# Splitting the second product's weights one group later, and making three operands before the second layer begins

## The chip, the cores and the metric

The kernel runs on one core of a Trainium2 chip. The metric is the device time of one execution in microseconds (us). Five engines work side by side, each through its own queue in order: TensorE (PE, with its weight loads shown as PEld), VectorE (DVE), ScalarE (ACT), GpSimd (POOL) and SyncE (SP), which issues nearly all DMAs. They meet through semaphores.

## The reference

The input passes through three layers:

```python
def _attn_ref(q, k, v, w_phi):           # linear attention, 4 x 8 heads of 576 x 64
    ...
    return (num / den).astype(np.float32)
def _moe_ref(x, w_in, w_out):            # 2304 x 512, d_ff 2048: the first layer below
    h = x @ w_in
    return np.maximum(0.01 * h, h) @ w_out
def _moe2_ref(x, domain_probs, w1, w2):  # 4 experts, F = 1024: the second layer below
    p = domain_probs / (domain_probs.sum(-1, keepdims=True) + 1e-09)
    for e in range(4):
        h = np.maximum(x @ w1[e], 0.0)
        out += p[:, e:e + 1] * (h @ w2[e])
```

Everything is float32. Each float32 operand of a matmul is split in two parts, a rounded high part ("hi", made on ACT) and the rest ("lo", a subtraction on DVE or POOL), and a product is three matmuls: hi by hi, hi by lo, lo by hi.

## The kernel before, in words

**Layout in time.** Attention and the first layer run mixed over the 4 batches, ordered by a written plan and the planner's own estimate. The first layer's last group, `moe1_group(16)`, holds only its "down" products: 8 pieces of 12 matmuls. Then comes the second layer, 48 groups `group(k)`, k = 16 j + c: three blocks j of 768 tokens, in each 16 slices c of 256 columns of w1.

**A group.** The product x @ w1 of a slice is done as 7 products of half size instead of 8 (Strassen's scheme: sums of blocks of x, `x2_steps`, by sums of blocks of w1, `w2_sums`). `product(k, i, ...)` is 6 matmuls of 384 columns, into PSUM tiles X, V and Y; ACT copies X to Y (line 804) before product 2 goes on in X. `relu_hi` (ACT) and `relu_lo` (DVE) make the operand of the second product. This second product, `down(k - 1, i)`, i = 0 to 5, belongs to the group before and stands between the products of group k: 6 matmuls of 512 columns each, then an add into the output by DVE (line 774). PE's order in a group: products 1, 5, down 3, products 2, 6, down 4, products 3, 7, down 5, down 0, product 4, down 1, down 2. Everything in `kept(...)` keeps the order in which it is written on its engine; DMAs and the first layer's work are placed by the planner.

**Weights of the first product.** `w2_dma` loads a slice of w1 (tile r), `w2_sums` makes 4 sums on POOL, `w2_hi` and `w2_lo` split them on ACT and POOL. This is done in group k for group k + 1.

**Weights of the second product.** `w2_dma_d` loads 2 x 256 KB of w2 into the tile r2, of which there is one (bufs 1). `w2_hi_d` (ACT, line 707) and `w2_lo_d` (POOL, line 711) split it into `wd[k]`, of which there are two (bufs 2). Before the change group k splits wd[k + 1], behind `relu_lo(k, 3, Z)` and ahead of down 5 of group k - 1. wd[k + 1] lies in the buffer of wd[k - 1], which down 3, 4, 5, 0, 1 and 2 of group k - 1 read in this same group.

**Sums of x.** A block needs 7 operands, in `XOPS` order b11, t1, b21, t2, b22, t3, t4. Those called b are split as they are; those called t need a subtraction first (line 616), then the hi part (ACT, line 638) and the lo part (line 639). For blocks 1 and 2 the subtractions run on POOL, one operand as the `fill` of groups c = 1, 3, 5, 7, 9, 11 and 15 of the block before. For block 0 they run on DVE: four are spread over the last batch of the first layer, b22 stands in the first layer's last group, and t3 and t4 (`extra`) inside group 0. Group 0 has no down products.

Of the kernel before, what the change touches and what calls it, by code (L numbers as in the profile page):

```python
# [75 lines left out]
NC2 = NE * FF2 // 256  # L76
# [3 lines left out]
def body(ctx, tc, kT, qT, vh, w_phi, w_in, w_out, probs, w1, w2, out):  # L80
# [504 lines left out]
    def pieces(*halves):  # L585

        cuts = sorted({0, TH} | {S - t0 % S for t0 in halves if S - t0 % S < TH})
        return [
            (o, e - o, [((t0 + o) // S, (t0 + o) % S) for t0 in halves])
            for o, e in zip(cuts, cuts[1:])  # L590
        ]
# [3 lines left out]
    def x2_steps(j):  # L595

        T = (2 * TH * j, 2 * TH * j + TH)
        kind = ([xp, xp, xp, 0, 0], [0, xp, xp, xp, xp], [xp, xp, xp, 0, 0])[j]
        slots, raw = [], []
        xops[j] = {}  # L600

        def half(i):
            if i % 3 == 0:
                pool = kind[i // 3] or x2p[0]
                slots.append(pool.tile([128, 3, 2, TH], F32R, tag="x", name="xo"))
            return slots[i // 3][:, i % 3]

        def part(d, t, o, n):
            b, s = t
            return accs[b][:, 2 * d : 2 * d + 2, s : s + n]  # L610

        eng = nc.vector if j == 0 else nc.gpsimd

        def diff(out, f, g, halves):
            for o, n, at in pieces(*halves):
                kept(eng.tensor_tensor(
                    out=out[:, :, o : o + n], in0=f(o, n, at), in1=g(o, n, at), op=ALU.subtract
                ))

        def step(i, name):  # L620
            if name[0] == "t":
                if not raw:
                    raw.append((x2p[0] if j else xp).tile([128, 3, 2, TH], F32, tag="x", name="xt"))
                r = raw[0][:, {"t1": 0, "t2": 1, "t3": 2, "t4": 0}[name]]
                of = {
                    "t1": (lambda o, n, at: part(0, at[1], o, n), lambda o, n, at: part(0, at[0], o, n), T),
                    "t2": (lambda o, n, at: part(1, at[0], o, n), lambda o, n, at: raw[0][:, 0, :, o : o + n], T[1:]),
                    "t3": (lambda o, n, at: part(1, at[0], o, n), lambda o, n, at: part(0, at[0], o, n), T[1:]),
                    "t4": (lambda o, n, at: part(1, at[0], o, n), lambda o, n, at: raw[0][:, 1, :, o : o + n], T[:1]),
                }[name]  # L630
                diff(r, *of)
                src = [(0, TH, r)]
            else:
                d, t = int(name[1]) - 1, T[int(name[2]) - 1]
                src = [(o, n, part(d, at[0], o, n)) for o, n, at in pieces(t)]
            hi, lo = half(2 * i), half(2 * i + 1)
            for o, n, r in src:
                kept(nc.scalar.copy(out=hi[:, :, o : o + n], in_=r))
                kept(eng.tensor_tensor(
                    out=lo[:, :, o : o + n], in0=r, in1=hi[:, :, o : o + n].bitcast(F32), op=ALU.subtract  # L640
                ))
            xops[j][name] = hi, lo

        return [lambda i=i, name=name: step(i, name) for i, name in enumerate(XOPS)]
# [8 lines left out]
    def kept(ins):  # L653

        if "h" in m2:
            tc.keep_in_program_order(ins)
        return ins
# [4 lines left out]
    def w2_dma(c):  # L662

        pool, tag = (m2["r"], "r") if m2 else (wp, "w")
        r = pool.tile([128, 4, 256], F32, tag=tag, name="r")
        nc.sync.dma_start(out=r[:, 2:4].rearrange("p a f -> p (a f)"), in_=w1[2 * c])
        nc.sync.dma_start(out=r[:, 0:2].rearrange("p a f -> p (a f)"), in_=w1[2 * c + 1])
        return r

    def w2_sums(r):  # L670
        pool, tag = (m2["r"], "r") if m2 else (wp, "w")
        s = pool.tile([128, 4, 256], F32, tag=tag, name="rs")
        for o, x, y, op in (
            (s[:, 0], r[:, 0], r[:, 1], ALU.add),
            (s[:, 1], s[:, 0], r[:, 2], ALU.subtract),
            (s[:, 2], r[:, 2], r[:, 0], ALU.subtract),
            (s[:, 3], r[:, 3], s[:, 1], ALU.subtract),
        ):
            kept(nc.gpsimd.tensor_tensor(out=o, in0=x, in1=y, op=op))  # L679
        return s  # L680

    def w2_dma_d(c):
        r2 = m2["r2"].tile([128, 2, DM], F32, tag="r2", name="r2")
        for t in range(2):
            nc.sync.dma_start(out=r2[:, t], in_=w2[2 * c + t])
        return r2

    def w2_operands(k):
        if m2:
            wo[k] = [m2["wu"].tile([128, 7, 256], F32R, tag="wu", name=n) for n in ("wuh", "wul")]  # L690
        else:
            wo[k] = [xp.tile([128, 7, 256], F32R, tag="x", name=n) for n in ("wuh", "wul")]
# [12 lines left out]
    def w2_hi_d(k, r2):  # L705
        wd[k] = m2["wd"].tile([128, 2, 2, DM], F32R, tag="wd", name="wd")
        kept(nc.scalar.copy(out=wd[k][:, 0], in_=r2))  # L707

    def w2_lo_d(k, r2):
        d = wd[k]  # L710
        kept(nc.gpsimd.tensor_tensor(out=d[:, 1], in0=r2, in1=d[:, 0].bitcast(F32), op=ALU.subtract))  # L711
# [19 lines left out]
    def relu_hi(k, at, src):  # L731
        kept(nc.scalar.activation(out=gs2[k][0][:, at], in_=src, func=AF.Relu))  # L732
# [46 lines left out]

        return evict  # L780

    def group(k, r, r2, fill, extra):

        gs2[k] = [m2["h"].tile([128, 4, TH], F32R, tag="h", name=n) for n in ("gh", "gl")]
        X = m2["px"].tile([128, 512], F32, tag="x", name="px")[:, 0:TH]
        V = m2["pv"].tile([128, 512], F32, tag="v", name="pv")[:, 0:TH]
        Z = m2["pz"].tile([128, 512], F32, tag="z", name="pz")[:, 0:TH]  # L790
        Y = m2["y"]
        ss = m2["sum"].tile([128, 2, TH], F32, tag="s", name="s")
        if k == 0:

            kept(nc.tensor.matmul(
                Y, lhsT=wo[k][0][:, 1, 0:128], rhs=xops[0]["b11"][0][:, 0], start=True, stop=True
            ))
        more = r is not None
        run = lambda f: f and f()
        if more:  # L800
            s = w2_sums(r)
            w2_operands(k + 1)
        product(k, 1, X, True)
        kept(nc.scalar.copy(out=Y, in_=X))  # L804
        product(k, 5, V, True)
        kept(nc.scalar.copy(out=ss[:, 0], in_=V))
        if more:
            w2_hi(k + 1, r, s, 0)
            w2_lo(k + 1, r, s, 0)
        run(down(k - 1, 3))  # L810
        for f in extra[:1]:
            f()
        product(k, 2, X, False)
        relu_hi(k, 0, X)
        relu_lo(k, 0, X)
        product(k, 6, Y, False)
        kept(nc.scalar.copy(out=ss[:, 1], in_=Y))
        if more:
            w2_hi(k + 1, r, s, 1)
            w2_lo(k + 1, r, s, 1)  # L820
        run(down(k - 1, 4))
        for f in extra[1:]:
            f()
        product(k, 3, V, False)
        kept(nc.vector.tensor_tensor(out=V, in0=V, in1=ss[:, 1], op=ALU.add))
        relu_hi(k, 1, V)
        product(k, 7, Y, False)
        kept(nc.vector.tensor_tensor(out=Z, in0=Y, in1=ss[:, 0], op=ALU.add))
        relu_lo(k, 1, V)
        relu_hi(k, 3, Z)  # L830
        relu_lo(k, 3, Z)
        if more:
            w2_hi_d(k + 1, r2)
            w2_lo_d(k + 1, r2)
        run(down(k - 1, 5))
        run(down(k - 1, 0))
        run(fill)
        product(k, 4, Y, False)
        relu_hi(k, 2, Y)
        relu_lo(k, 2, Y)  # L840
        run(down(k - 1, 1))
        run(down(k - 1, 2))
# [12 lines left out]
    for b in range(B):  # L855
# [5 lines left out]
        else:  # L861
            early = x2_steps(0)
# [11 lines left out]
    r = w2_dma(0)  # L874
# [3 lines left out]
        w2_hi(0, r, s, i)  # L878
        w2_lo(0, r, s, i)
    for i, f in enumerate(G[2:]):  # L880
        if i == 2:
            early[4]()
        f()
    left0.close()
    for name, bufs in (("r", 2), ("r2", 1), ("wu", 4), ("wd", 2), ("sum", 2), ("h", 4)):
# [3 lines left out]
        m2[name] = opened(left, name, bufs, space=bass.MemoryType.PSUM)  # L889
    m2["y"] = m2["py"].tile([128, 512], F32, tag="y", name="py")[:, 0:TH]  # L890
    n = NB * NC2
    r2 = w2_dma_d(0)
    r = w2_dma(1)
    w2_hi_d(0, r2)
    w2_lo_d(0, r2)
    nxt = []
    for k in range(n):
        j, c = divmod(k, NC2)
        if c == 0 and j + 1 < NB:
            nxt = x2_steps(j + 1)  # L900
        r2 = w2_dma_d((k + 1) % NC2) if k + 1 < n else None
        fill = nxt.pop(0) if nxt and (c % 2 == 1 and c < 12 or c == NC2 - 1) else None
        group(k, r, r2, fill, early[5:] if k == 0 else [])
        r = w2_dma((k + 2) % NC2) if k + 2 < n else None
    for i in (3, 4, 5, 0, 1, 2):
        down(n - 1, i)()
    left.close()
# [34 lines left out]
```

## Time and profile before

| | us |
|---|---|
| median of 3 runs | 1461.37 |
| lowest and highest | 1460.64, 1462.51 |
| the profiled execution's own time | 1460.94 |
| its span in the trace | 1459.2 |
| first matmul of the second layer, from the span's start | 641.08 |

The busy shares of the whole span are PE 94%, DVE 56%, ACT 45% and POOL 39%; the mean granted clock of PE is 0.975 of full speed. These are means over stages with different limits, so the rows below are taken stage by stage. The second layer is read in windows of one group each, from the first matmul of product 1 to that of the next group. In a timeline row the first number is the start from the span's start, the second the duration in us, and the bracket the idle time of that engine before it with what ended it.

### The profile page before, as it was taken

The page shows a single profiled execution, that of the slowest core. Times are in us where ns is not written, and L with a number is a line of the kernel's source. Part 1 is how long each engine was busy: PE and PEld are TensorE (multiplying, and loading weights), DVE is VectorE, ACT ScalarE, POOL GpSimd, SP SyncE. Part 2 cuts the span into 40 slices and gives each one's busy share as a digit, 9 for nine tenths or more (in the row PEclk, how much of TensorE's full clock was granted, in tenths as well). Part 3 has the DMA queues.
Part 4 walks back from the last instruction along what each step waited for, and adds up shares of the span by engine and source line. Part 5 has one row for each costly group of instructions (what it writes and reads, how often), then busy time and mean ns, then how long its engine had stood idle before and what let it go on. Part 6 is the DMA issues. An engine that isn't in the chain of part 4 may idle for free.

```text
span 1459.2 us, 21227 instructions
## 1 busy us (share of the span) xinstructions
PE 1375.0 (94%) x8105; PEld 1278.9 (88%) x8105; DVE 810.1 (56%) x1285; ACT 658.9 (45%) x1201; POOL 569.8 (39%) x398
## 2 busy tenths in 40 slices
PE   8869989999999999979898989898998989999998
PEld 6658989999999999969787878787887979999997
DVE  5369889778776566544344434444444435445445
ACT  5447656676566345333343433333343333343341
POOL 3212102111110000045565755655666565566561
PEclk9979999999999999999999999999999999999999
DMA  6347544343332222121121212211212113122121
GB/s 210 102 150 268 210 165 146 108 121 98 112 97 68 82 88 87 58 72 58 58 72 51 75 50 73 101 58 59 71 50 68 59 65 109 59 73 73 58 73 44
DMA packets 78039, 134.95 MB, mean 92 GB/s; under 512 B 11760, under 2 KB 22128, under 8 KB 77936
## 3 DMA queue, kind: packets, MB, share of 16 engines
q1 hardware_dynamic: 77936, 133.58, 28.4%
q8 instruction: 64, 1.05, 0.3%
q14 instruction: 39, 0.32, 0.1%
HBM read 120.30 MB, written 13.18 MB: 91 GB/s over the span
## 4 chain that ended last, share of the span: by engine, by line
PE 75%; DMA 6%; POOL 5%; DVE 5%; issue 5%; ACT 2%; SPq 0%; ACTq 0%; POOLq 0%; DVEq 0%
PE po L758 24%; PE op L535 12%; PE hp L503 11%; PE py L719 9%; PE px L719 6%; PE pv L719 5%; PE kvp L242 3%; PE nm L335 2%; DMA rb<-dr 2%; POOL wul L701 2%; POOL wd L711 2%; DMA qraw<-qT 1%; PE pk L204 1%; DMA w<-w 1%; POOL rs L679 1%
## 5 line engine op out<-in xcount | busy, mean ns | idle before, releaser
L758 PE MATMUL po<-wd,gh 128*128 128x512 f32 x1152 | 389.5, 393 | 0.0
L758 PEld LDWEIGHTS po<-wd,gh 128*128 128x128 f32 x1152 | 218.2, 189 | 41.6
L774 DVE SCALAR_TENSOR_TENSOR ob<-po,pe,ob 128x512 f32<-128x512 f32 x270 | 196.9, 747 | 93.0 <-PE po L758 90.1
L711 POOL TENSOR_TENSOR wd<-r,wd 128x1024 fp32r<-128x1024 f32 x48 | 115.3, 2402 | 302.8 <-ACT wd L707 302.8
L535 PE MATMUL op<-gt,wt 128*128 128x288 f32 x1536 | 222.8, 299 | 6.8 <-DVE g L517 5.6
L758 PE MATMUL po<-wd,gl 128*128 128x512 f32 x576 | 227.2, 394 | 0.0
L296 POOL PARTITION_ALL_REDUCE mb<-pc x32 | 76.8, 2404 | 370.8 <-ACT pc L294 294.3
L503 PE MATMUL hp<-xh,wt 128*128 128x288 f32 x1024 | 216.4, 298 | 4.8 <-ACT xh L117 4.8
L535 PEld LDWEIGHTS op<-gt,wt 128*128 128x128 f32 x1536 | 210.4, 190 | 8.5 <-DVE g L517 6.0
L503 PEld LDWEIGHTS hp<-xh,wt 128*128 128x128 f32 x1024 | 167.8, 189 | 5.8 <-ACT xh L117 5.1
L707 ACT CAST wd<-r 128x1024 fp32r<-128x1024 f32 x48 | 50.4, 1050 | 266.8 <-PE po L758 253.1
L736 DVE SCALAR_TENSOR_TENSOR gl<-py,gh 128x384 fp32r<-128x384 f32 x48 | 26.8, 558 | 258.1 <-ACT gh L732 258.1
L719 PE MATMUL py<-xo,wuh 128*128 128x384 f32 x576 | 153.8, 349 | 7.5 <-ACT gh L732 7.4
L503 PE MATMUL hp<-xl,wt 128*128 128x288 f32 x512 | 152.4, 298 | 0.1
L679 POOL TENSOR_TENSOR rs<-r 128x256 f32<-128x256 f32 x96 | 71.4, 744 | 174.6 <-DMA r<-w 174.6
L719 PE MATMUL px<-xo,wuh 128*128 128x384 f32 x384 | 105.6, 358 | 35.6 <-ACT py L804 35.5
L758 PEld LDWEIGHTS po<-wd,gl 128*128 128x128 f32 x576 | 109.0, 189 | 15.4
L719 PEld LDWEIGHTS py<-xo,wuh 128*128 128x128 f32 x576 | 109.7, 196 | 11.7 <-ACT gh L732 7.7
L701 POOL TENSOR_TENSOR wul<-rs,wuh 128x1024 fp32r<-128x1024 f32 x48 | 115.3, 2403 | 5.3 <-ACT wuh L696 5.3
L719 PEld LDWEIGHTS px<-xo,wuh 128*128 128x128 f32 x384 | 73.4, 198 | 47.9 <-ACT py L804 41.7
L719 PE MATMUL py<-xo,wul 128*128 128x384 f32 x288 | 99.8, 347 | 0.0
L719 PE MATMUL pv<-xo,wuh 128*128 128x384 f32 x384 | 99.0, 339 | 0.0
(114 smaller groups left out, 2417.4 us busy)
## 6 DMA issues: line engine op xcount, KB each, us to landing
r<-w SPq DMA_DIRECT2D x192, 256.0 KB, 2.7
wr<-w SPq DMA_DIRECT2D x96, 256.0 KB, 3.3
qraw<-qT SPq DMA_DIRECT2D x32, 288.0 KB, 7.1
r<-w_out SPq DMA_DIRECT2D x9, 1024.0 KB, 9.2
r<-w_in SPq DMA_DIRECT2D x8, 1024.0 KB
w<-w SPq DMA_DIRECT2D x32, 256.0 KB, 2.1
v<-vh SPq DMA_DIRECT2D x16, 480.0 KB, 4.1
kraw<-kT SPq DMA_DIRECT2D x16, 288.0 KB, 5.9
```

The costliest lines, as they stand in the source:

```text
L242: nc.tensor.matmul(kvp[:, a * 128 : (a + 1) * 128], lhsT=lhs, rhs=v[:, c, h * D : h * D + 128], start=(c == 0), stop=(c == 4),)
L296: nc.gpsimd.partition_all_reduce(mb, pc, 128, bass_isa.ReduceOp.absmax)
L335: nc.tensor.matmul(o, lhsT=a[:, 2 * (h % 2) + j], rhs=x[:, j * HS : (j + 1) * HS], start=(j == 0 and i == 0), stop=(j == 1 and i == len(P) ...
L503: nc.tensor.matmul(hp[:, n, 0:HS], lhsT=wi[:, a, kk * 128 : (kk + 1) * 128], rhs=x[z][:, kk, n * HS : (n + 1) * HS], start=(kk == 0 and i ...
L535: nc.tensor.matmul(op[:, n, 0:HS], lhsT=wt1[1, C * GF + f][:, a, d * 128 : (d + 1) * 128], rhs=gts[C * GF + f][:, z, n * HS : (n + 1) * HS ...
L679: kept(nc.gpsimd.tensor_tensor(out=o, in0=x, in1=y, op=op))
L701: kept(nc.gpsimd.tensor_tensor(out=lo[:, at], in0=(r[:, 1:4], s)[i], in1=hi[:, at].bitcast(F32), op=ALU.subtract))
L707: kept(nc.scalar.copy(out=wd[k][:, 0], in_=r2))
L711: kept(nc.gpsimd.tensor_tensor(out=d[:, 1], in0=r2, in1=d[:, 0].bitcast(F32), op=ALU.subtract))
L719: kept(nc.tensor.matmul(out, lhsT=ws[w][:, AOPS[a], kk * 128 : (kk + 1) * 128], rhs=xo[z][:, kk], start=first and n == 0, stop=n == 5, ski ...
L758: kept(nc.tensor.matmul(op, lhsT=(gh, gl)[z][:, 2 * f + t, q : q + 128], rhs=d[:, w, f], start=n == 0, stop=n == 5,))
L774: kept(nc.vector.scalar_tensor_tensor(out=o, in0=op, scalar=ps, in1=o, op0=ALU.mult, op1=ALU.add))
```

## The change

The split of wd moves by one group: group k now splits wd[k] instead of wd[k + 1], at the same place in its order, so that the buffer written is that of wd[k - 2]. The loads follow: r2 for group k + 1 is asked for after group k and after the request for r; before, it was asked for ahead of group k. wd[0] is split in group 0 instead of ahead of it. The other part: t3 and t4 of block 0 are made in the first layer's last group, and `extra` goes.

```diff
-    def group(k, r, r2, fill, extra):
+    def group(k, r, r2, fill):
...
         run(down(k - 1, 3))
-        for f in extra[:1]:
-            f()
         product(k, 2, X, False)
...
         run(down(k - 1, 4))
-        for f in extra[1:]:
-            f()
         product(k, 3, V, False)
...
         relu_lo(k, 3, Z)
-        if more:
-            w2_hi_d(k + 1, r2)
-            w2_lo_d(k + 1, r2)
+        w2_hi_d(k, r2)
+        w2_lo_d(k, r2)
         run(down(k - 1, 5))
...
     for i, f in enumerate(G[2:]):
-        if i == 2:
-            early[4]()
+        if i in (1, 2, 3):
+            early[3 + i]()
         f()
...
+    r = w2_dma(1)
     r2 = w2_dma_d(0)
-    r = w2_dma(1)
-    w2_hi_d(0, r2)
-    w2_lo_d(0, r2)
     nxt = []
     for k in range(n):
...
+        fill = nxt.pop(0) if nxt and (c % 2 == 1 and c < 12 or c == NC2 - 1) else None
+        group(k, r, r2, fill)
+        r = w2_dma((k + 2) % NC2) if k + 2 < n else None
         r2 = w2_dma_d((k + 1) % NC2) if k + 1 < n else None
-        fill = nxt.pop(0) if nxt and (c % 2 == 1 and c < 12 or c == NC2 - 1) else None
-        group(k, r, r2, fill, early[5:] if k == 0 else [])
-        r = w2_dma((k + 2) % NC2) if k + 2 < n else None
```

## Rows read from the trace of the kernel before

**Rows 1.** Waits of PE, 640 us to the end: who waited for whom, total us, times, longest.
```profile
PE px L719 <- ACT py L804: 35.5, 9, 4.5
PE py L719 <- ACT gh L732: 7.4, 1, 7.4
```

**Rows 2.** Windows: length, busy us (instructions) by engine, PE's granted clock, DMA share, GB/s.
```profile
690.68:706.32 15.64, 15.64 (x79) 14.14 (x78) 7.49 (x12) 6.04 (x10) 9.39 (x7) 1.00 0.20 68
641.36:658.59 17.23, 9.04 (x44) 8.13 (x44) 8.22 (x10) 7.83 (x12) 11.22 (x8) 0.84 0.33 110
658.59:674.80 16.21, 16.21 (x80) 14.72 (x79) 6.17 (x10) 5.07 (x9) 8.73 (x7) 0.96 0.20 65
...
1128.30:1132.00 3.70, 3.70 (x12) 3.70 (x13) 1.81 (x3) 1.45 (x3) 3.62 (x6) 0.50 0.00 0
```

**Rows 3.** Windows of groups 4, 8, 12, 16, 20, 24, 28, 32: their sum.
```profile
sum 176.72, PE 141.89 PEld 126.67 DVE 59.20 ACT 54.07 POOL 103.94; mean PE 17.74 PEld 15.83 DVE 7.40 ACT 6.76 POOL 12.99
```

**Rows 4.** Windows of groups 2, 6, 10, 18, 22, 26: their sum.
```profile
sum 95.33, PE 95.24 PEld 84.45 DVE 44.61 ACT 40.19 POOL 67.58; mean PE 15.87 PEld 14.08 DVE 7.43 ACT 6.70 POOL 11.26
```

**Rows 5.** Timeline, end of group 3 (fill t1) and first half of group 4.
```profile
699.12 2.40 POOL L701 TENSOR_TENSOR wul<-rs,wuh 128x1024 fp32r<-128x1024 f32 x1
...
700.56 0.49 ACT L732 ACTIVATE gh<-pz 128x384 fp32r<-128x384 f32 x1 [0.50 <-DVE pz L828]
...
706.57 1.05 ACT L707 CAST wd<-r 128x1024 fp32r<-128x1024 f32 x1 [5.52 <-PE po L758]
...
707.70 2.39 POOL L711 TENSOR_TENSOR wd<-r,wd 128x1024 fp32r<-128x1024 f32 x1 [6.17 <-ACT wd L707]
...
708.90 0.62 PE L758 MATMUL po<-wd,gh 128*128 128x512 f32 x2
...
709.58 0.39 PE L758 MATMUL po<-wd,gh 128*128 128x512 f32 x1
710.04 1.80 POOL L616 TENSOR_TENSOR xt<-acc 128x768 f32<-128x768 f32 x1
...
711.87 0.83 ACT L638 CAST xo<-xt 128x768 fp32r<-128x768 f32 x1 [4.25 <-POOL xt L616]
...
713.77 0.46 ACT L804 COPY py<-px 128x384 f32<-128x384 f32 x1 [0.68 <-DVE gl L736]
...
714.29 0.89 PE L719 MATMUL px<-xo,wuh 128*128 128x384 f32 x2 [4.33 <-ACT py L804]
```

**Rows 6.** Timelines of SP, ACT, POOL, DVE, PE: group 0.
```profile
640.37 0.36 SPq L666 DMA_DIRECT2D r<-w  x1
...
642.87 1.05 ACT L707 CAST wd<-r 128x1024 fp32r<-128x1024 f32 x1 [13.62 <-DMA r<-w]
...
645.07 0.83 ACT L696 CAST wuh<-r 128x768 fp32r<-128x768 f32 x1 [0.37 <-DMA r<-w]
...
646.34 0.74 POOL L679 TENSOR_TENSOR rs<-r 128x256 f32<-128x256 f32 x1
...
650.53 1.80 POOL L701 TENSOR_TENSOR wul<-r,wuh 128x768 fp32r<-128x768 f32 x1
650.60 1.04 ACT L696 CAST wuh<-rs 128x1024 fp32r<-128x1024 f32 x1 [3.20 <-POOL rs L679]
...
652.29 2.34 POOL L701 TENSOR_TENSOR wul<-rs,wuh 128x1024 fp32r<-128x1024 f32 x1
...
652.41 3.03 DVE L639 TENSOR_TENSOR xo<-xt,xo 128x768 fp32r<-128x768 f32 x1 [3.11 <-ACT xo L638]
...
656.53 0.98 PE L719 MATMUL py<-xo,wuh 128*128 128x384 f32 x2 [7.44 <-ACT gh L732]
```

**Rows 7.** Groups by form, DVE, from 620 us: busy, mean ns, idle before.
```profile
L548 DVE TENSOR_TENSOR acc<-op,acc 128x576 f32<-128x576 f32 x5 | 3.8, 756 | 5.9 <-PE op L535 5.9
```

**Rows 8.** Timeline of DVE at 560 us.
```profile
560.28 0.96 DVE L639 TENSOR_TENSOR xo<-xt,xo 128x768 fp32r<-128x768 f32 x1 [0.17 <-ACT xo L638]
```

**Rows 9.** DMA issues: count, KB each, median us from issue to landing.
```profile
r<-w SPq DMA_DIRECT2D x192, 256.0 KB, 2.7
```

## The prediction, written before the changed kernel ran

> **What bounds the kernel now.** I read the windows of the second layer first, one per group, then the waits of PE, then the timeline around the longest wait. The change touches only the second layer and the last group ahead of it, so what lies before that can be left aside.
>
> A group in which nothing goes wrong takes 15.64 us, with PE busy from end to end at a granted clock of 1.00 [rows 2]. Its 36 matmuls of 512 columns start 0.227 us apart (three from 708.90 to 709.58 [rows 5]), 8.2 us in all, and leave 7.4 us for the 42 matmuls of the seven products. That is a floor that the change doesn't lower; it can only bring other groups down to it. Three kinds stand above it. Eight groups sum to 176.72 us [rows 3], which is 176.72 - 8 x 15.64 = 51.6 us too much. Six more sum to 95.33 us [rows 4], 1.5 us too much. Group 0, with no down products, takes 17.23 us where its seven products need 7.4, and group 1 takes 16.21 [rows 2].
>
> The waits say who is late: PE waited 35.5 us for ACT's copy of X (line 804), and 7.4 us once for a relu [rows 1]. The eight long groups are those behind a group with a t fill (c = 3, 7, 11, 15, for two blocks). Rows 5 show one such place, to be read backwards: PE resumes at 714.29, released by the copy at 713.77; ACT came late to it because it sat 4.25 us waiting for POOL's subtraction of x, ended at 711.84; POOL began that at 710.04 only because the lo part of wd kept it until then; and that waited for the hi part on ACT, which had sat 5.52 us until PE's last down of the group before let the buffer of wd go. The matmuls of the copied tile are due when down 3 ends, at 709.58 + 0.23 = 709.81. The wait is thus about 4.3 us of the excess; the rest (51.6 / 8 = 6.4 us a group) comes from the clock behind it: after group 28's wait PE ran at 0.50 of the full clock, the 1.2 GHz level, for at least 3.7 us [rows 2], so it lost half of that, 1.9 us.
>
> **The change part by part.** *The split of wd.* Count and size stay: 48 casts of 1.05 us and 48 subtractions of 2.39 us [rows 5]. Only the buffer differs. wd[k] lies where wd[k - 2] was, whose last reader is the down 2 that ends group k - 1, so at its place in group k the cast finds a free buffer. In rows 5's group ACT is through with `relu_hi(k, 3, Z)` at 700.56 + 0.49 = 701.05; the cast runs to 702.10; POOL has ended its own lo part at 699.12 + 2.40 = 701.52, so it makes wd's lo from 702.1 to 704.5. Now it ends at 710.09: POOL's subtraction of x comes 5.6 us earlier. From the start of that subtraction to PE's resumption is now 714.29 - 710.04 = 4.25 us. From 704.5 the same chain (1.80 subtraction, 0.83 cast, relu, its lo part, copy) ends at 708.75, and PE wants it at 709.81. It is hidden with 1.06 us to spare. Product 4's relu also waits in this queue behind the fill's cast, as it does now, but its input is there by then. I take the whole 51.6 us off. Bounds: at best 51.6; at worst the chain comes 2 us later than this, so that PE waits 1 us and pays up to another 1 us to the slow clock in each of eight groups, 35.6.
>
> The six groups behind a b fill lose 0.25 us by the same late cast; the fill's casts then come at once, and 1.5 us go (bounds 0 and 1.5).
>
> What is late next in such a group is wd's lo part for the next group's down 3, whose third matmul (the first to read it) starts at 708.90; it ends at 704.5, so 4.4 us are left in every group, fill or not. Behind it on POOL stand the four sums of the next slice, which come earlier than today.
>
> *The loads.* The r2 request leaves when `w2_lo_d` frees the one buffer, now in the same group instead of the next, and stands on SP behind the request for r, which waits for the lo part that POOL makes before wd's. Nothing on SP turns the order round. Where a block's six outputs are stored, both requests stand behind the stores, but have some 10 us until the next cast of wd. The new wait, ACT's cast for r2, has behind it the relu of product 4 and the copy of X. The loop is lo part 2.39, two issues of 0.36 [rows 6], landing 2.7 [rows 9], cast 1.05: 6.9 us of 15.64. Cost nothing.
>
> *The start.* t3 and t4 are out of group 0, and so is wd[0] ahead of it: six ACT, DVE and POOL steps of 0.5 to 3 us, no DMA. Now group 0's last product waits 7.44 us [rows 6] at the end of a chain: w1's sums on POOL, ACT's cast of them (3.20 us idle before it), t4's cast behind that, t4's lo part on DVE, 3.03 us long, and the add that frees Y behind it. Without it PE runs six products from 641.36 to about 647.7, waits some 0.8 us for the add that reads Y (an estimate: a DVE step of 384 columns, 0.5 us by the 0.756 that 576 take [rows 7], and two hand-overs), and ends the group at about 649.5. Then POOL sets the pace, for it has everything for group 1 to do. The request for r goes first on SP instead of behind r2's; it left at 640.37 and had landed by 645.07 [rows 6], so I put it 0.9 us sooner, at 644.1. POOL: four sums of 0.74, lo parts of 1.80 and 2.40, wd 2.40: done at 647.1, 648.9, 651.3 and 653.7. Group 1's product 1 is not held; product 5 reaches its first lo weights at about 650.95 and waits 0.35; down 3 reaches wd's lo at 652.45 and waits 1.25. So groups 0 and 1 take 7.4 + 15.6 + 0.8 + 0.35 + 1.25 = 25.4 us instead of 33.44: 8.0 us off. Bounds: 10.4 with no wait at all; 5.2 with r as late as now (0.9) and one spell of slow clock (1.9).
>
> *The last group of the first layer.* t3 and t4 add two subtractions and two lo parts, each about 0.96 us long [rows 8], on DVE, and two casts of 0.83 on ACT. ACT idles 13.62 us there [rows 6], DVE 5.9 us between its evictions [rows 7], against 3.9 us of new work; the planner may even put the two subtractions far earlier, their inputs being old. Free in my sum. At worst the last eviction, for which PE waits at the seam, comes one step late: 1 us.
>
> Rows 6 and 8 show what the place is worth: t4's lo part took 3.03 us beside POOL's subtraction of 652.29 to 654.63, and the same form 0.96 alone; 3.03 is just POOL's remaining 2.22 plus 0.8. The Trainium skill (SBUF — State Buffer, "Who interferes with whom") says that a DVE instruction with two SBUF inputs is held until a GpSimd instruction that reads SBUF is over; the trace agrees with those 3.03 us. It speaks against the move if the planner places these steps among POOL's split of w1, ahead of the first layer's last lo part, for which PE waits: by it one POOL step of 2.4 us would be added to the start and the sum would be 58.7 instead of 61.1. At the place written, POOL idles until group 0, and I take nothing.
>
> **Sum.** 51.6 + 1.5 + 8.0 = 61.1 us. The profiled execution took 1460.94 us (span 1459.2 and 1.7 around it), which gives 1399.8; the median shown is 0.4 above it, so 1400.3 us.
>
> **The rivals.** *The start gives little* (15 in 100). POOL is the bottleneck from 644 to 654 and could be worse off than worked out; for it, 3.20 us of ACT idle behind POOL's sums even now; against it, these waits are at most 3 us. The start is then worth 0 to 5 us, the time 1403 to 1408.
>
> *The t groups keep part of their wait* (7 in 100). POOL still does wd's lo part ahead of the subtraction of x, and the margin is 1.06 us. For it, that margin; against it, POOL's durations hardly vary. With a loss of 2 to 2.6 us in eight groups, 1416 to 1421.
>
> *The cast still waits in each group* (3 in 100): the change of buffer doesn't do what it says, because another operand is late. Then only the start is gained, 1453.
>
> *Slower: the single r2 buffer becomes the bound* (3 in 100). lo part, request, landing, cast must go round once per group. It decides from a landing 12.1 us after the lo part (15.64 - 2.39 - 1.05); every us above that is paid 47 times. A landing after 13.6 us costs 47 x 1.5 = 70 us, so 1471. For it, one buffer and a request now behind another; against it, the median of 2.7 us [rows 9].
>
> **How the numbers follow.** The forecast has 72 in 100; its own range, from the bounds, is 1397 (61.1 plus 2.4 at the start and a little more) to 1404. The range that should hold the time 8 times in 10 reaches over the first rival and part of the way to the second: 1396 to 1412. About 0.2%, 3 us, is what a measurement of this kernel tells from no change. All cases but the last are faster by more than that; I keep 0.01 for no difference and 0.03 for slower, so 0.96 for faster.
>
> **What would show it.** In the profile after, the cast of line 707 shows no idle time from PE's down; the subtractions of line 616 start about 5.5 us sooner in their group; the wait of PE for line 804's copy is gone or below 3 us in total; all groups from 2 to 46 last 15.6 to 15.7 us at clock 1.00; group 0 lasts 8 to 9 us, and group 1 shows short waits for POOL's lo parts. It would be wrong if PE waited for wd (line 711) in the plain groups, or if the copy of X still came behind a waiting ACT.

## The result and the profile after

The changed kernel takes 1397.61 us (median of 4 runs, 1396.92 to 1398.86) against 1461.94 us of the kernel before (4 runs on the same chip): a ratio of 0.956, 95% interval 0.9543 to 0.9577. The forecast was 1400.3 us. The profiled execution took 1398.86 us with a span of 1397.1 us; mean granted clock of PE 0.989 instead of 0.975.

Windows of the kernel after, one group each (columns as in [rows 2]): groups 0, 1, 3 and 4.

```profile
640.98:649.23 8.25, 7.59 (x43) 7.27 (x43) 2.71 (x5) 5.16 (x9) 5.79 (x6) 1.00 0.39 128
649.23:666.07 16.84, 15.94 (x79) 14.03 (x79) 7.48 (x12) 7.54 (x13) 14.89 (x11) 1.00 0.34 108
681.71:697.35 15.64, 15.64 (x79) 14.14 (x78) 6.39 (x10) 5.55 (x10) 9.50 (x6) 1.00 0.19 66
697.35:712.99 15.64, 15.64 (x79) 14.15 (x78) 8.81 (x14) 7.20 (x12) 13.05 (x11) 1.00 0.22 71
```

Group 4 is now as long as a plain group and at full clock. The sums of the windows of the eight groups of [rows 3], and then of the six of [rows 4]:

```profile
sum 124.96, PE 124.96 PEld 113.13 DVE 70.41 ACT 57.56 POOL 104.38; mean PE 15.62 PEld 14.14 DVE 8.80 ACT 7.20 POOL 13.05
```

```profile
sum 93.72, PE 93.72 PEld 84.85 DVE 46.06 ACT 36.06 POOL 67.54; mean PE 15.62 PEld 14.14 DVE 7.68 ACT 6.01 POOL 11.26
```

From 176.72 to 124.96 is 51.8 us; from 95.33 to 93.72, 1.6 us. Groups 0 and 1 go from 33.44 to 25.09 us, 8.35 us. Together with a second layer that begins 0.4 us sooner (its first matmul, a single one ahead of product 1, at 640.69 instead of 641.08) this is the 62.1 us by which the spans differ.

The waits of PE from 640 us to the end, after (to be held against [rows 1]):

```profile
PE po L758 <- POOL wd L711: 0.9, 1, 0.9
PE py L795 <- DVE acc L548: 0.9, 1, 0.9
PE py L719 <- DVE pz L824: 0.7, 1, 0.7
```

The timeline of the kernel after where [rows 5] stand, group 3 with the fill t1 and the start of group 4 (group 4 starts at 697.35 here, at 706.32 in the kernel before):

```profile
689.00 2.40 POOL L701 TENSOR_TENSOR wul<-rs,wuh 128x1024 fp32r<-128x1024 f32 x1 [1.79 <-ACT wuh L696]
...
691.59 0.49 ACT L732 ACTIVATE gh<-pz 128x384 fp32r<-128x384 f32 x1
...
691.97 1.04 ACT L707 CAST wd<-r 128x1024 fp32r<-128x1024 f32 x1
...
693.09 2.39 POOL L711 TENSOR_TENSOR wd<-r,wd 128x1024 fp32r<-128x1024 f32 x1 [1.69 <-ACT wd L707]
...
695.44 1.84 POOL L616 TENSOR_TENSOR xt<-acc 128x768 f32<-128x768 f32 x1
...
697.32 0.84 ACT L638 CAST xo<-xt 128x768 fp32r<-128x768 f32 x1 [4.30 <-POOL xt L616]
...
699.22 0.46 ACT L804 COPY py<-px 128x384 f32<-128x384 f32 x1 [0.68 <-DVE gl L736]
...
699.93 0.62 PE L758 MATMUL po<-wd,gh 128*128 128x512 f32 x2
...
700.83 0.51 PE L719 MATMUL px<-xo,wuh 128*128 128x384 f32 x2
```

The cast of wd follows the relu without a gap. ACT waits for POOL's subtraction as long as before (4.30 us), yet the chain behind it ends at 699.68 with the copy of X, before PE wants it at 700.83. This long wait on an engine off the path costs nothing: only its end counts.

The start of the second layer, after:

```profile
628.77 1.56 ACT L638 CAST xo<-xt 128x768 fp32r<-128x768 f32 x2
...
631.62 1.81 DVE L639 TENSOR_TENSOR xo<-xt,xo 128x768 fp32r<-128x768 f32 x2
633.36 0.74 DVE L548 TENSOR_TENSOR acc<-op,acc 128x576 f32<-128x576 f32 x1
...
639.87 0.33 SPq L666 DMA_DIRECT2D r<-w  x1
...
643.37 0.74 POOL L679 TENSOR_TENSOR rs<-r 128x256 f32<-128x256 f32 x1 [13.22 <-DMA r<-w]
...
648.08 0.62 PE L719 MATMUL py<-xo,wuh 128*128 128x384 f32 x2 [0.66 <-DVE pz L824]
...
650.41 2.41 POOL L711 TENSOR_TENSOR wd<-r,wd 128x1024 fp32r<-128x1024 f32 x1
...
652.87 0.73 PE L758 MATMUL po<-wd,gh 128*128 128x512 f32 x2 [0.90 <-POOL wd L711]
```

The casts and lo parts of t3 and t4 run while ACT and DVE have room, each lo part in about 0.95 us; POOL begins on w1's sums at 643.37, when r lands, instead of 646.34.

### The profile page after: what moved, and what is told of

Same layout as the page of the kernel before. It is cut to its first block, busy times and chain, and to the rows that moved or that the text cites. A ratio compares the mean times of both kernels' runs of the same rounds, so it can differ in the third digit from the quotient of the medians.

```text
span 1397.1 us, 21274 instructions
## 1 busy us (share of the span) xinstructions
PE 1355.4 (97%) x8105; PEld 1264.4 (91%) x8105; DVE 816.9 (58%) x1285; ACT 658.4 (47%) x1201; POOL 572.7 (41%) x398
## 3 DMA queue, kind: packets, MB, share of 16 engines
q8 instruction: 64, 1.05, 0.3%
## 4 chain that ended last, share of the span: by engine, by line
PE 86%; DMA 6%; DVE 4%; issue 2%; ACT 1%; POOL 0%; SPq 0%; DVEq 0%; ACTq 0%; POOLq 0%
PE po L758 28%; PE op L535 13%; PE hp L503 12%; PE py L719 11%; PE pv L719 7%; PE px L719 7%; PE kvp L242 4%; PE nm L335 2%; DMA rb<-dr 2%; DMA qraw<-qT 2%; PE pk L204 2%; DMA w<-w 1%; DMA r<-w_in 1%; PE pq L292 1%; DVE w L461 1%
## 5 line engine op out<-in xcount | busy, mean ns | idle before, releaser
L774 DVE SCALAR_TENSOR_TENSOR ob<-po,pe,ob 128x512 f32<-128x512 f32 x270 | 201.6, 749 | 216.5 <-PE po L758 216.5
L719 PE MATMUL py<-xo,wuh 128*128 128x384 f32 x576 | 148.2, 338 | 0.7 <-DVE pz L824 0.7
L701 POOL TENSOR_TENSOR wul<-r,wuh 128x768 fp32r<-128x768 f32 x48 | 88.9, 1851 | 84.9 <-ACT wuh L696 84.9
L719 PEld LDWEIGHTS py<-xo,wuh 128*128 128x128 f32 x576 | 104.9, 188 | 4.6 <-DVE pz L824 1.0
L719 PE MATMUL px<-xo,wuh 128*128 128x384 f32 x384 | 98.6, 338 | 0.0
L503 PEld LDWEIGHTS hp<-xl,wt 128*128 128x128 f32 x512 | 96.4, 188 | 1.1 <-DVE xl L118 0.7
L804 ACT COPY py<-px 128x384 f32<-128x384 f32 x48 | 22.2, 463 | 143.6 <-PE px L719 137.5
```

The source lines that it names most:

```text
L503: nc.tensor.matmul(hp[:, n, 0:HS], lhsT=wi[:, a, kk * 128 : (kk + 1) * 128], rhs=x[z][:, kk, n * HS : (n + 1) * HS], start=(kk == 0 and i ...
L701: kept(nc.gpsimd.tensor_tensor(out=lo[:, at], in0=(r[:, 1:4], s)[i], in1=hi[:, at].bitcast(F32), op=ALU.subtract))
L719: kept(nc.tensor.matmul(out, lhsT=ws[w][:, AOPS[a], kk * 128 : (kk + 1) * 128], rhs=xo[z][:, kk], start=first and n == 0, stop=n == 5, ski ...
L774: kept(nc.vector.scalar_tensor_tensor(out=o, in0=op, scalar=ps, in1=o, op0=ALU.mult, op1=ALU.add))
```

## The experiments

The theory: in the eight groups PE pays for the order of POOL's queue, wd's lo part standing late and ahead of the subtraction of x, and for the slow clock behind the wait. The rival: PE pays for ACT's wait for the buffer of wd in itself. Beside this, what each part is worth, and how much spare time is left.

### One part at a time

**Only the split of wd moved.** t3 and t4 stay in group 0. Its edit against the changed kernel:

```diff
-        if i in (1, 2, 3):
-            early[3 + i]()
+        if i == 2:
+            early[4]()
...
+        for f in extra[:1]:      # behind down 3; extra[1:] behind down 4
+            f()
```

> The new split of wd alone; t3 and t4 stay in group 0. Theory (the eight long groups are POOL's lo part of wd standing, late, ahead of the subtraction of x): all groups from 2 to 46 last 15.6 us at clock 1.00, so 53 us go as in the full change. Group 0 still waits for t4, but w1's sums start some 2 us sooner on POOL, so groups 0 and 1 take about 30 us instead of 33.4. Time 1404 to 1407. Rival (the two parts need each other, or the start is worth nothing by itself): long groups remain, or 1398.

Measured: 1402.39 us, ratio 0.9599 (0.9584 to 0.9613). Its windows of groups 0, 1, and 2 to the end:

```profile
640.13:651.77 11.64, 7.85 (x43) 7.37 (x43) 6.49 (x10) 6.82 (x11) 9.13 (x6) 0.98 0.44 134
651.77:668.79 17.02, 17.02 (x80) 15.54 (x80) 7.48 (x12) 7.26 (x13) 13.65 (x10) 0.91 0.24 74
668.79:1395.91 727.12, 727.12 (x3625) 657.07 (x3623) 355.87 (x558) 284.27 (x473) 467.47 (x341) 1.00 0.22 71
```

From group 2 on PE is busy without a gap and takes 727.12 us, as in the full change. Groups 0 and 1 take 28.66 us, so moving the split alone gives 4.8 us at the start, where I expected 3.4, and the time falls below my range; t3 and t4 give 3.6 us on top. What t4 costs here can be read from DVE, POOL and PE in its group 0:

```profile
645.89 1.02 DVE L616 TENSOR_TENSOR xt<-acc,xt 128x768 f32<-128x768 f32 x1
646.06 2.53 POOL L701 TENSOR_TENSOR wul<-r,wuh 128x768 fp32r<-128x768 f32 x1
...
647.95 1.46 DVE L639 TENSOR_TENSOR xo<-xt,xo 128x768 fp32r<-128x768 f32 x1 [1.03 <-ACT xo L638]
...
649.33 0.55 DVE L825 TENSOR_TENSOR pv<-pv,s 128x384 f32<-128x384 f32 x1
...
650.49 0.60 PE L719 MATMUL py<-xo,wuh 128*128 128x384 f32 x2 [3.79 <-ACT gh L732]
```

Most of it is t4's place in DVE's queue. V's add (line 825 here) stands behind t4's lo part and starts 9.2 us into the group, where it starts at 5.5 us in the changed kernel. The add that frees Y for PE's last product comes behind it, and PE waits 3.79 us (its row names a relu that ends within 0.1 us of that add). A smaller part is that DVE and POOL slow each other: POOL's lo part takes 2.53 us where 1.80 is usual, and DVE's 1.46 instead of 0.96.

**Only t3 and t4 moved.** Against the kernel before:

```diff
-        if i == 2:
-            early[4]()
+        if i in (1, 2, 3):
+            early[3 + i]()
...
-        group(k, r, r2, fill, early[5:] if k == 0 else [])
+        group(k, r, r2, fill, [])
```

> t3 and t4 in the first layer's last group alone; wd is split as before. Theory: the eight long groups stay at 21.5 to 23 us and the six at 15.9; only groups 0 and 1 shrink, from 33.4 to about 26.3 us (POOL still has wd[0] ahead of w1's sums, 2.4 us). Time 1454 to 1456. Rival (t3 and t4 were what made group 0 long only together with wd[0]): above 1458.

Measured: 1453.15 us, ratio 0.9943 (0.9927 to 0.996). Windows of groups 0, 1 and 4, and the sum over the eight groups:

```profile
638.73:648.17 9.44, 7.85 (x43) 7.21 (x43) 1.69 (x3) 4.88 (x8) 6.54 (x6) 1.00 0.43 144
648.17:665.37 17.20, 16.18 (x80) 14.05 (x79) 7.20 (x12) 6.50 (x12) 12.16 (x9) 1.00 0.28 91
696.89:718.66 21.77, 17.44 (x79) 15.60 (x78) 7.39 (x12) 6.77 (x11) 12.98 (x9) 0.92 0.16 49
```

```profile
sum 177.05, PE 142.21 PEld 126.82 DVE 59.17 ACT 54.11 POOL 103.99; mean PE 17.78 PEld 15.85 DVE 7.40 ACT 6.76 POOL 13.00
```

The eight groups stay (177.05 us beside 176.72), the start falls to 26.64 us, near the 26.3 counted. At the start the parts overlap: 4.8 and 6.8 us alone, 8.35 us together, for both shorten the same wait ahead of group 0's last product. It was 7.44 us; 3.79 are left with the split alone, 0.7 with t3 and t4 alone.

### Which queue held PE up

**The fill first, in the kernel before.** One line moves; the cast of wd keeps its buffer and its wait.

```diff
+        run(fill)
         if more:
             w2_hi_d(k + 1, r2)
             w2_lo_d(k + 1, r2)
         run(down(k - 1, 5))
         run(down(k - 1, 0))
-        run(fill)
```

> The kernel before with one move: the fill stands ahead of the split of wd[k + 1] on ACT and POOL. The cast of wd still waits 5 us or so for PE's last down. Theory (the harm is the order, subtraction of x behind wd's lo part): POOL subtracts at once, the casts of x come at once, the copy of X is ready about 0.6 us before PE wants it, and the eight groups fall to 15.6 us though ACT waits as long as ever for the buffer: 53 us less, group 0 as before, 1408 to 1410. Rival (ACT's wait for the buffer is itself what PE pays for): the long groups stay, 1455 to 1462.

Measured: 1407.78 us, ratio 0.9633 (0.9619 to 0.9647). Its window of group 4, and ACT and POOL around its start:

```profile
704.08:719.72 15.64, 15.64 (x79) 14.14 (x78) 7.50 (x12) 6.04 (x10) 9.40 (x7) 1.00 0.24 69
```

```profile
699.25 1.85 POOL L616 TENSOR_TENSOR xt<-acc 128x768 f32<-128x768 f32 x1
701.14 0.83 ACT L638 CAST xo<-xt 128x768 fp32r<-128x768 f32 x1 [2.33 <-POOL xt L616]
...
704.32 1.05 ACT L707 CAST wd<-r 128x1024 fp32r<-128x1024 f32 x1 [2.35 <-PE po L758]
...
706.44 0.46 ACT L804 COPY py<-px 128x384 f32<-128x384 f32 x1 [0.68 <-DVE gl L736]
```

The cast of wd still starts when PE's last down releases the buffer, 0.24 us after the group's start at 704.08 (as at 706.57 and 706.32 in the kernel before), and no long group is left: from group 2 on PE takes 727.12 us without a gap, the same as in the full change. ACT's wait just ahead of the cast is 2.35 us here instead of 5.52, since it first waits for POOL and casts x. The rival falls: the late buffer alone costs PE nothing.

**Only POOL's order turned, in the kernel before.** wd's lo part goes behind the fill, its cast stays.

```diff
         if more:
             w2_hi_d(k + 1, r2)
-            w2_lo_d(k + 1, r2)
         run(down(k - 1, 5))
         run(down(k - 1, 0))
         run(fill)
+        if more:
+            w2_lo_d(k + 1, r2)
```

> The kernel before with only POOL's order turned: wd's lo part behind the fill, its hi part on ACT where it was. Theory: POOL subtracts x at once, but ACT's casts of x still stand behind the late cast of wd; counted from rows of before, cast of wd to 707.6, cast of x to 708.45, relu, lo part, copy of X ended at 710.1, which PE wants at 709.8. So each of the eight groups waits about 0.3 us, with or without a spell of slow clock: 1409 to 1417. Rival (ACT's wait for the buffer alone): 1455 to 1462.

Measured: 1411.2 us, ratio 0.9659 (0.9643 to 0.9675). ACT and PE's weight load around the start of its group 4, and the sum of the eight groups:

```profile
706.15 1.05 ACT L707 CAST wd<-r 128x1024 fp32r<-128x1024 f32 x1 [5.52 <-PE po L758]
707.11 0.82 ACT L638 CAST xo<-xt 128x768 fp32r<-128x768 f32 x1
...
709.00 0.46 ACT L804 COPY py<-px 128x384 f32<-128x384 f32 x1 [0.68 <-DVE gl L736]
...
709.51 0.30 PEld L719 LDWEIGHTS px<-xo,wuh 128*128 128x128 f32 x2 [0.39 <-ACT py L804]
```

```profile
sum 126.83, PE 126.83 PEld 112.56 DVE 58.50 ACT 52.49 POOL 89.70; mean PE 15.85 PEld 14.07 DVE 7.31 ACT 6.56 POOL 11.21
```

With POOL's order turned 49.9 of the 51.8 us are gone, though ACT waits 5.52 us as ever. What remains is 0.23 us a group: the cast of x behind the late cast of wd brings the copy just too late. The matmul rows show no gap; the weight load ahead of them does.

### How much room is left, and what a wait costs

Three kernels make POOL's subtraction in the t fills of the changed kernel longer by useless work (its output is the same).

```diff
                 diff(r, *of)
+                if j:                       # first: one extra piece of 128 x 384
+                    f, g, halves = of
+                    o, n, at = pieces(*halves)[0]
+                    kept(eng.tensor_tensor(
+                        out=r[:, :, 0:192], in0=f(0, 192, at), in1=g(0, 192, at), op=ALU.subtract
+                    ))
...
-                diff(r, *of)
+                for _ in range(2 if j else 1):   # second: twice; third: 3 times
+                    diff(r, *of)
```

> The changed kernel with a useless extra POOL subtraction of 128 x 384 (about 1.0 us) behind each of the eight t subtractions of blocks 1 and 2. Theory: the copy of X ends 1.09 us before PE wants it, so 1.0 us more is just hidden: no wait of PE, same time as the changed kernel within 1 us, 1397 to 1399. Rival (there is more slack than the rows show, or less): the three kernels of this series show where the wait begins.

> The changed kernel with the t subtraction of blocks 1 and 2 done twice (1.84 or 2.03 us more on POOL). Theory: a PE wait of 0.75 to 0.95 us in each of eight groups, 6 to 8 us in all, and if a wait this short brings no slow clock nothing more: 1404 to 1406. If it does bring the slow clock as the waits of 4.3 us did, up to 1.9 us more in each: 1420. Rival (slack is larger than 1.09): under 1400.

> The changed kernel with the t subtraction done three times (3.7 to 4.1 us more on POOL). Theory: a PE wait of 2.6 to 2.9 us in each of eight groups, 22 us, plus a spell at half clock as behind the waits of 4.3 us (1.6 to 2.9 us a group): 1432 to 1442. Without slow clock 1420.

Measured: 1400.06 us (ratio 0.9578, 0.9557 to 0.9598), 1407.43 us (0.9631, 0.9611 to 0.9651) and 1430.83 us (0.9793, 0.9765 to 0.982). The sums of the eight groups, in this order:

```profile
sum 126.04, PE 126.04 PEld 112.56 DVE 69.67 ACT 58.10 POOL 112.42; mean PE 15.76 PEld 14.07 DVE 8.71 ACT 7.26 POOL 14.05
```

```profile
sum 133.05, PE 127.19 PEld 112.58 DVE 69.67 ACT 58.07 POOL 119.19; mean PE 15.90 PEld 14.07 DVE 8.71 ACT 7.26 POOL 14.90
```

```profile
sum 154.37, PE 133.15 PEld 117.95 DVE 69.67 ACT 57.60 POOL 133.93; mean PE 16.64 PEld 14.74 DVE 8.71 ACT 7.20 POOL 16.74
```

Over the 124.96 us of the changed kernel these are 0.13, 1.01 and 3.68 us a group for 1.0, 1.9 and 3.8 us more on POOL. In the third, PE's busy time is 0.74 us a group above the second's (133.15 beside 127.19 us), which is slow clock; 2.9 us are left without it. So the room is about 0.9 us, and beyond it POOL's time is paid one to one. The first kernel's 1.1 us over eight groups are seen in the windows; its median lies 2.4 us above the changed kernel's, 1 us above my range, but the intervals of the two ratios overlap. In the second, PE's row in group 4 and the load ahead of it (lines 720 and 805 are 719 and 804 of the changed kernel):

```profile
702.57 0.30 PEld L720 LDWEIGHTS px<-xo,wuh 128*128 128x128 f32 x2 [1.09 <-ACT py L805]
702.58 0.62 PE L720 MATMUL px<-xo,wuh 128*128 128x384 f32 x2 [0.67 <-ACT py L805]
```

The eight waits of PE sum to 5.9 us, the groups grew by 8.1. A wait costs some 0.27 us more than the matmul's gap says: the weight load, in the changed kernel 0.22 us ahead of its matmul and beside the one before, starts together with it here. My forecast, 1404 to 1406 us, reckoned with gaps alone.

The third is the odd one. Windows of its groups 4 and 12, then 2 us of each from just behind the wait:

```profile
698.24:718.03 19.79, 17.21 (x79) 15.37 (x78) 8.71 (x14) 7.15 (x12) 16.71 (x13) 0.91 0.18 58
831.92:850.42 18.50, 15.92 (x79) 14.08 (x78) 8.71 (x14) 7.25 (x12) 16.66 (x13) 1.00 0.18 57
704.60:706.50 1.90, 1.90 (x6) 1.90 (x7) 1.23 (x2) 0.94 (x2) 1.82 (x4) 0.50 0.03 9
838.20:840.20 2.00, 2.00 (x12) 2.00 (x13) 1.48 (x3) 1.51 (x3) 1.92 (x4) 1.00 0.03 8
```

Both groups wait the same 2.58 us. Behind one PE runs at 0.50, the 1.2 GHz level, behind the other at 1.00. Four of the eight groups pay the slow clock (1.3 to 1.6 us more of PE's busy time each), four don't. I had expected all, hence 1432 us as the lower end.

### The last wait of the start

**wd[0]'s lo part on DVE.**

```diff
-        kept(nc.gpsimd.tensor_tensor(out=d[:, 1], in0=r2, in1=d[:, 0].bitcast(F32), op=ALU.subtract))
+        eng = nc.vector if k == 0 else nc.gpsimd
+        kept(eng.tensor_tensor(out=d[:, 1], in0=r2, in1=d[:, 0].bitcast(F32), op=ALU.subtract))
```

> The changed kernel with wd[0]'s lo part on DVE instead of POOL, group 0 alone. Theory: group 1's wait of 0.90 us for POOL goes and perhaps the 0.3 us of matmul behind it, so groups 0 and 1 take 24 us instead of 25.1; DVE's step reads two tiles of SBUF beside POOL's lo part of w1 and is held until that ends, some 2 us, so the relu's lo part behind it comes late but in time. Time 1396 to 1397, too little for the comparison to tell; the windows would show it. Rival: DVE held up makes PE wait elsewhere, no gain.

Measured: 1398.18 us, ratio 0.9565 (0.9545 to 0.9585), not to be told from the changed kernel's 0.956. Windows of groups 0 and 1, and DVE's row:

```profile
639.94:648.19 8.25, 7.59 (x43) 7.27 (x43) 2.71 (x5) 5.15 (x9) 5.95 (x6) 1.00 0.37 126
648.19:663.83 15.64, 15.64 (x79) 14.15 (x79) 9.25 (x13) 7.57 (x13) 12.38 (x10) 1.00 0.36 114
```

```profile
648.49 1.85 DVE L712 TENSOR_TENSOR wd<-r,wd 128x1024 fp32r<-128x1024 f32 x1 [0.39 <-ACT wd L707]
```

Group 1 falls from 16.84 to 15.64 us, the floor. That is 1.2 us shown in the windows and too little for the medians. DVE's step took 1.85 us in all, so it was not held for the 2 us that I expected. It leaves 0.66 us ahead of product 4 as the only wait of PE inside the groups.

## Why the prediction was right, point by point

**The eight groups.** Predicted 51.6 us off, measured 51.8. The steps held one by one: the cast follows the relu, POOL's subtraction starts 1.91 us ahead of the next group instead of 3.72 behind its start, 5.6 us sooner, as worked out. The spare time was put at 1.06 us; by the copy's end it is 1.1, by the lengthened kernels 0.9, since PE's weight load is due ahead of the matmul. The spell of slow clock behind the wait went with it, as counted. The two order kernels show the cause: a free buffer (the change) or the fill in front of the cast (the first of them) each removes the wait, so it took the late buffer and the order behind it together to hold PE up.

**The six groups.** Predicted 1.5 us, measured 1.6.

**The start.** Predicted 25.4 us for groups 0 and 1, measured 25.09. The waits come where they were put: 0.66 ahead of product 4 (0.8 predicted), none at product 5 (0.35), 0.90 at down 3's third matmul (1.25), which makes group 1 1.2 us too long. The term that was mis-sized is the landing of r: counted from the first matmul of product 1, POOL's sums begin after 2.39 us (640.98 to 643.37), where 2.74 were put (641.36 to 644.1).

**The moved sums of x.** Free, as forecast. The planner put both subtractions far ahead (the later one starts at 561.6 us) and the rest between ACT's and DVE's older work; the first eviction follows at 633.36, and PE doesn't wait for it. POOL's holding DVE up, which spoke against the move, did not come about, since the lo parts ran when POOL was idle; the kernel that leaves t4 in group 0 shows DVE's lo part 0.5 us longer beside POOL.

**The rivals.** None came. The one r2 buffer never held the cast up: it waited for nothing in any of 48 groups. Wd's lo part ends at 695.48, its reader comes at 699.93, so 4.4 us are free, as forecast. In the rival of the single r2 buffer a subtraction was off: 15.64 - 2.39 - 1.05 is 12.2, not 12.1, so its 70 us would be 66, and 1471 would be 1466; nothing else hangs on it.

**The sum.** 1399.8 us were predicted for the profiled execution, 1398.86 came. The 0.9 us are 0.3 at the start, 0.3 for the middle block's groups of 15.60 us, which I took at 15.64, and the first layer ending 0.4 us sooner, which was luck: nothing in the prediction asked for it. The medians differ by 64.3 us, 3.2 more than the 61.1 predicted. About 1 us of that is the difference just named; for the rest, the profiled execution lies 1.2 us above the median after and 1.0 us below it before, and that was not traced further. Between the executions profiled here the second layer's first matmul lies anywhere from 638.45 to 641.71 us, a spread that I didn't trace to any of the edits: differences of 1 or 2 us are to be read in windows of the second layer. Seven of the eight experiments' medians lie outside the ranges that I gave for them, by 0.2 to 1.6 us; the readings above rest on the windows and waits.

## What to carry to other kernels

Here a cast that waited for a buffer did no harm by its own idle time. Look at what stands behind it in its queue, and behind its consumer's queue, and whether that is wanted before the buffer is free. Where a buffer is released late, either place the step where its slot is already free or put the work that is wanted first in front: here each alone removed the wait. Price such a wait from the end of the chain, by the first instruction that PE needs from it, and add the weight load and, where rows show it, the spell of slow clock behind.

## What the runs showed of the hardware

The slow clock behind a wait isn't settled by the wait's length: in the kernel with the subtraction done three times, 2.6 to 2.8 us brought it in four of eight groups, with equal waits of 2.58 us on both sides, while 4.3 to 4.5 us brought it in all eight groups of the kernel before, and 0.7 to 0.9 us in none of the eight groups of the kernel with the subtraction done twice. What decides between equal waits stays open. The Trainium skill (TensorE: Matmul & The Clock Gate, "Part 1: The HAM clock gate") says that the chip watches activity in a free-running way, which does not start with the kernel's work; that would let equal waits fall differently, and no run here shows it.

DVE and POOL steps that read two SBUF tiles each lengthened one another in both directions in group 0 of the kernel with only the split moved: POOL's lo part took 2.53 instead of 1.80 us where DVE had begun 0.2 us earlier, and DVE's 1.46 instead of 0.96 where POOL had.
